# Two value products, the scale of x and its split moved one step earlier in a fused attention and two-layer-pair kernel

## The chip, the cores and the metric

The kernel runs on one core of one Trainium2 chip. The metric is the device time of one execution in microseconds (us); the kernel before takes 1294.16 us (median of three runs, 1293.89 to 1294.37). TensorE (PE) does the matrix products, ScalarE (ACT) and VectorE (DVE) the work on their results, GpSimd (POOL) part of the subtractions, and SyncE (SP) issues the DMAs.

## The reference

An attention of 12,288 query tokens over 768 keys, which serve as values too, is followed by two feed-forward pairs of width 2048:

```
kv_pool = kv.reshape(B, H // r, r, W // r, r, C).mean(axis=(2, 4))
k = v = kv_pool.reshape(B, -1, C) @ w_sr
a = softmax(q @ k.T / sqrt(C));   x = a @ v
h = x @ w_in;   g = max(h, 0) + alpha * min(h, 0);   x = g @ w_out
h = x @ w_in2;  g = h * sigmoid(1.702 * h);          out = g @ w_out2
```

C is 128, so q and x have 128 columns. All is float32 at the surface.

## The kernel before, in words

Every float32 operand is split in two float16 parts, high and low, and each product is three matmuls (high by high, high by low, low by high), all recorded at lines 103, 104 and 105. Ahead of a split a power of two is found from the largest absolute value, so that the parts keep their precision.

The 12,288 tokens are 24 blocks of 512, numbered 0 to 23. A block's 2048 hidden columns are 16 pieces of 128. One loop over steps t runs all blocks as a pipeline, 16 steps to a block. Block j's first layer stands at steps 16j to 16j+15, one piece in each; its second layer comes 4 steps later, the third 31 and the fourth 36 steps later. A step in the middle of the program thus works on three or four blocks at once. The text uses these short names:

- L1 m, L2 m, L3 m, L4 m: the three matmuls of piece m in one of the four layers. L1 and L3 write a tile `h` in PSUM, L2 and L4 add up in a tile `y`.
- A1 m (line 346) and A3 m (line 401): the ScalarE function on `h`. D1 m (line 347) and D3 m (line 402): the VectorE operation behind it, the last reader of that `h`. H1 m (354) and H3 m (409): ScalarE's cast to the high part. P1 m (355) and P3 m (411): the subtraction that gives the low part, on GpSimd, or on VectorE for P3 of every fourth piece.
- S n: the scores of the next block's n-th tile of 128 queries (lines 236 to 240). The work behind it is a maximum on VectorE (`nm`, line 245), the exponential on ScalarE (255), the scaled high part `ah` on ScalarE (269), the low part `al` on VectorE (280), and a DMA transpose of each.
- V k: the k-th of six products with the values, which add up x in the PSUM tile `xacc`.

Between V 5 and the first layer of the same block stands the chain that this case is about. `top_of` reduces `xacc` on VectorE (`ta`, line 304) and writes a column `xd`. `x_scale` has TensorE spread `xd` over the partitions with a matmul of one column (`pt`, line 309), and VectorE makes the scale `xc` of it (`xp`, `xc`). `x_split` writes the high part `xh` on ScalarE (320) and the low part `xl` on VectorE (321). L1 0 of the block reads `xh` and `xl`.

The matmul `pt` writes a tile of the same PSUM pool `ps_h` as L1 and L3. It has three buffers, handed out in the order in which the code asks for them. So `pt` takes a place in that row, and the L1 and L3 that stand around it need the buffers of pieces that are nearer to them.

Which step holds what is written in tables: `ATT_START` gives the step at which a block's attention begins (16j-25 for block j), `ATT_S` the places of its four S, `ATT_V` those of its six V, and the loop in `step` has the lags of `x_scale` and `x_split`. The code of the steps is then ordered once more by a scheduler that moves an instruction ahead where it expects the one before it to wait. Each engine gets a fixed list and works it in that order; an instruction that waits holds all behind it on its engine.

The lines that the change touches:

Of the kernel before, what the change touches and what calls it, by code (L numbers as in the profile page):

```python
# [27 lines left out]
KF = DFF // P  # L28
TB = 512
NB = NTOK // TB  # L30
# [7 lines left out]
L2_LAG, L3_LAG, L4_LAG = 4, 31, 36  # L38

ATT_START = [-18, -5] + [KF * j - 25 for j in range(2, NB)]  # L40
ATT_S = [(0, 2, 2, 6), (0, 3, 6, 9)] + [(0, 4, 7, 12)] * (NB - 2)
ATT_V = [(5, 8, 9, 12), tuple(range(12, 18))] + [(17, 18, 19, 21, 22, 22)] * (NB - 2)
KV_FREE = -11
W4_LOAD = -8

# [8 lines left out]
def attn_moe_kernel(ctx: ExitStack, tc: tile.TileContext, q, kv, w_sr, w_in1, w_out1, alpha, w_in2, w_out2, out):  # L54
# [47 lines left out]
    def mm3(o, wh, wl, xh, xl, start, stop):  # L102
        mm(out=o, lhsT=wh, rhs=xh, start=start, stop=False)  # L103
        mm(out=o, lhsT=wh, rhs=xl, start=False, stop=False)  # L104
        mm(out=o, lhsT=wl, rhs=xh, start=False, stop=stop)  # L105
# [7 lines left out]
    def small(name, dt=F32, w=1):  # L113
        return sm_p.tile([P, w], dt, tag=name, name=name)
# [90 lines left out]
    def flush():  # L205
        while late:
            late.pop(0)()
# [3 lines left out]
    def a_q(j):  # L211
        d = small("qd", BF16)
        top_of(q_t[j], d)
        qsc[j] = d

    def q_split(j):
        src = q_t.pop(j)
        qh[j] = at_p.tile([P, TB], F16, tag="qh", name="qh")
        ql[j] = at_p.tile([P, TB], F16, tag="ql", name="ql")
        c, p = scale_of(qsc[j], ps_x.tile([P, TB], F32, tag="x", name="qt"), None, "q")  # L220
        qsc[j] = p
        late.append(lambda: parts(qh[j], ql[j], src, c))
# [27 lines left out]
    def a_e(j, t):  # L250
        d = st[j, t]

        e = e_p.tile([P, 2, HALF], F32, tag="e", name="e") if j < 2 else d["s"][:, :, 0:HALF]
        sm = at_p.tile([P, 1], F32, tag="sm", name="sm")
        nc.scalar.activation(e, d["s"][:, :, 0:HALF], AF.Exp, bias=d["nm"], scale=qsc[j], accum_out=sm)  # L255
        r = at_p.tile([P, 1], F32, tag="r", name="r")
        d["e"], d["r"] = e, r

        def f():

            nc.vector.tensor_scalar(out=r, in0=sm, scalar1=1e-9, scalar2=2.0 ** -15, op0=ALU.add, op1=ALU.mult)
            nc.vector.reciprocal(out=r, in_=r)

        late.append(f)

    def a_h(j, t):
        d = st[j, t]
        d["ah"] = e_p.tile([P, 2, HALF], F16, tag="ah", name="ah")
        nc.scalar.activation(d["ah"], d["e"], AF.Copy, scale=d["r"])
        if t == 0:  # L270
            eh[j] = at_p.tile([P, KT, TB], F16, tag="eh", name="eh")
            el[j] = at_p.tile([P, KT, TB], F16, tag="el", name="el")
        nc.sync.dma_start_transpose(out=eh[j][:, :, t * P:(t + 1) * P], in_=d["ah"].rearrange("p h k -> p (h k)"))

    def a_l(j, t):
        d = st.pop((j, t))
        lo = e_p.tile([P, 2, HALF], F16, tag="al", name="al_")

        def f():
            nc.vector.scalar_tensor_tensor(out=lo, in0=d["e"], scalar=d["r"], in1=d["ah"], op0=ALU.mult, op1=ALU.subtract)  # L280
            nc.sync.dma_start_transpose(out=el[j][:, :, t * P:(t + 1) * P], in_=lo.rearrange("p h k -> p (h k)"))

        late.append(f)

    def a_v(j, k):
        if k == 0:
            xacc[j] = ps_x.tile([P, TB], F32, tag="x", name="xacc")
        if j == 0:

            ts_ = slice(k * P, (k + 1) * P)  # L290
            for i in range(KT):
                mm3(xacc[j][:, ts_], v_hi[:, i, :], v_lo[:, i, :], eh[j][:, i, ts_], el[j][:, i, ts_],
                    i == 0, i == KT - 1)
        else:
            mm3(xacc[j], v_hi[:, k, :], v_lo[:, k, :], eh[j][:, k, :], el[j][:, k, :], k == 0, k == KT - 1)
        if k == len(ATT_V[j]) - 1:
            d = small("xd", BF16)
            xsc[j] = d
            late.append(lambda: top_of(xacc[j], d))
# [36 lines left out]
    def l1(j, m):  # L336
        h = ps_h.tile([P, TB], F32, tag="h", name="h1")
        ms = slice(m * P, (m + 1) * P)
        mm3(h, wh["w1"][:, ms], wl["w1"][:, ms], xh[j], xl[j], True, True)
        h1[j, m] = h  # L340
# [9 lines left out]
    def l1_split(j, m):  # L350
        hi = g_p.tile([P, TB], F16, tag="g1h", name="g1h")
        lo = g_p.tile([P, TB], F16, tag="g1l", name="g1l")
        g = gg.pop((j, m, 1))
        nc.scalar.copy(hi, g)  # L354
        nc.gpsimd.tensor_tensor(out=lo, in0=g, in1=hi, op=ALU.subtract)  # L355
        g1[j, m] = hi, lo

    def l2(j, m):
        if m == 0:
            y1[j] = ps_y.tile([P, TB], F32, tag="y", name="y1")  # L360
        hi, lo = g1.pop((j, m))
        ms = slice(m * P, (m + 1) * P)
        mm3(y1[j], wh["w2"][:, ms], wl["w2"][:, ms], hi, lo, m == 0, m == KF - 1)
        if m == KF - 1:
            y = y1.pop(j)
            yc[j] = at_p.tile([P, TB], F32, tag="yc", name="yc", bufs=1)
            d = small("yd", BF16)
            ysc[j] = d

            def f():  # L370

                nc.scalar.copy(yc[j], y)
                top_of(y, d)

            late.append(f)
# [21 lines left out]
    def l3_act(j, m):  # L397
        h = h3.pop((j, m))
        g = t_p.tile([P, TB], F32, tag="g2", name="g2", bufs=3)

        nc.scalar.activation(g, h, AF.Tanh, scale=ysc[j][:, 0:1])  # L401
        nc.vector.scalar_tensor_tensor(out=g, in0=g, scalar=1.0, in1=h, op0=ALU.add, op1=ALU.mult)  # L402
        gg[j, m, 2] = g

    def l3_split(j, m):
        hi = g_p.tile([P, TB], F16, tag="g2h", name="g2h")
        lo = g_p.tile([P, TB], F16, tag="g2l", name="g2l")
        g = gg.pop((j, m, 2))
        nc.scalar.copy(hi, g)  # L409
        e = nc.vector if j == 0 or m % 4 == 3 or j == NB - 1 and m % 2 else nc.gpsimd  # L410
        e.tensor_tensor(out=lo, in0=g, in1=hi, op=ALU.subtract)  # L411
        g2[j, m] = hi, lo

    def l4(j, m):
        if m == 0:
            y2[j] = ps_y.tile([P, TB], F32, tag="y", name="y2")
        hi, lo = g2.pop((j, m))
        ms = slice(m * P, (m + 1) * P)
        mm3(y2[j], wh["w4"][:, ms], wl["w4"][:, ms], hi, lo, m == 0, m == KF - 1)
        if m == KF - 1:  # L420
            ob = t_p.tile([P, TB], F32, tag="ob", name="ob")
            y = y2.pop(j)
            u = ysc.pop(j)

            def f():
                nc.scalar.activation(ob, y, AF.Copy, scale=u[:, 1:2])
                nc.sync.dma_start(out=out[:, j * TB:(j + 1) * TB], in_=ob)

            late.append(f)
# [104 lines left out]
    def at(t, lag):  # L534

        j, m = divmod(t - lag, KF)
        return (j, m) if 0 <= j < NB else None

    def step(t):
        pieces = [(j, t - ATT_START[j]) for j in range(NB) if -8 < t - ATT_START[j] < 26]  # L540
        if x := at(t, L2_LAG):
            l2(*x)
        flush()
        if x := at(t, 2):
            l1_split(*x)
        if x := at(t, L3_LAG + 1):
            l3_act(*x)
        if x := at(t, L3_LAG + 2):
            l3_split(*x)
        if x := at(t, 0):  # L550
            l1(*x)
        if x := at(t, L4_LAG):
            l4(*x)
        flush()
        for j, p in pieces:
            for n, p0 in enumerate(ATT_S[j]):
                if p == p0 + 1:
                    a_e(j, n)
                elif p == p0 + 2:
                    a_h(j, n)  # L560
                elif p == p0 + 3:
                    a_l(j, n)
        flush()
        for j, p in pieces:
            for n, p0 in enumerate(ATT_S[j]):
                if p == p0:
                    a_s(j, n)
            for k, p0 in enumerate(ATT_V[j]):
                if p == p0:
                    a_v(j, k)  # L570
            if p == -6 and j > 0:
                a_q(j)
            if p == -4 and j > 0:
                q_split(j)
                late.append(lambda j=j: q_scale(j))
                if j + 1 < NB:
                    load_q(j + 1)
        for f, lag in ((x_scale, -2), (x_split, -1), (y_scale, L2_LAG + KF), (y_split, L2_LAG + KF + 2)):
            if (x := at(t, lag)) and x[1] == 0:
                f(x[0])  # L580
        if x := at(t, L3_LAG):
            l3(*x)
        if x := at(t, 0):
            l1_act(*x)
        flush()
# [59 lines left out]
```

## Time and profile before

| | |
|---|---|
| time, median of 3 runs | 1294.16 us |
| the profiled execution: time, span | 1294.28 us, 1292.5 us |
| TensorE busy | 1228.2 us, 95% of the span |
| VectorE, ScalarE, GpSimd busy | 1036.0, 1107.2, 780.6 us |
| mean granted TensorE clock | 0.979 of full speed |

TensorE is busy nearly all the time after a start of some 150 us, and the other engines have gaps. But the length that the profile gives a matmul (0.38 us for 512 columns) overlaps the next one: a row of 512 columns starts 0.216 us after the one before it where nothing holds it. A wait of less than the overlap does not show as idle time; it shows as a start that is further from the last start than that. So the waits of the middle are read from the starts in the timeline, not from the table of waits.

### The profile page before, as it was taken

What the parts mean: (1) busy time and instruction counts of PE and PEld (TensorE: products, weight loads), DVE (VectorE), ACT (ScalarE), POOL (GpSimd) and SP (SyncE); (2) the same over time, 40 slices, a digit from 0 to 9 for tenths busy, and PEclk for the clock granted to TensorE, in tenths of its full rate; (3) what the DMA queues carried; (4) which work ended last, traced back from release to release, by engine and by line L of the source; (5) the groups of instructions that cost most, each with busy time, mean ns of one, the idle gap of its engine ahead of it and who ended that gap; (6) DMA issues with size and microseconds to landing.
All of it is one profiled execution on the core that took longest, in us unless ns stands there. A gap on an engine that the chain in (4) does not pass through costs nothing.

```text
span 1292.5 us, 18032 instructions
## 1 busy us (share of the span) xinstructions
PE 1228.2 (95%) x5784; PEld 567.1 (44%) x5784; DVE 1036.0 (80%) x1879; ACT 1107.2 (86%) x1964; POOL 780.6 (60%) x670
## 2 busy tenths in 40 slices
PE   3468999999999999999999999999999999999998
PEld 2323444444444444444444444444444444444443
DVE  7988899778788787887887787787888878877666
ACT  1477899899898898898898998998988988988998
POOL 1046535576675676666665665756756666667774
PEclk8678999999999999999999999999999999999999
DMA  9713312122121221211221121221212212110000
GB/s 374 169 43 56 62 33 54 37 41 54 25 54 42 37 54 33 45 42 37 48 48 38 42 54 30 49 47 32 53 33 46 49 32 43 34 37 21 9 9 17
DMA packets 165375, 66.65 MB, mean 52 GB/s; under 512 B 156448, under 2 KB 156576, under 8 KB 164256
## 3 DMA queue, kind: packets, MB, share of 16 engines
q1 hardware_dynamic: 165280, 65.51, 21.9%
q8 instruction: 45, 0.74, 0.2%
q14 instruction: 50, 0.41, 0.1%
HBM read 21.05 MB, written 6.29 MB: 21 GB/s over the span
## 4 chain that ended last, share of the span: by engine, by line
PE 55%; ACT 16%; DVE 13%; issue 5%; DMA 0%; POOLq 0%; ACTq 0%
PE h L103 8%; PE h L105 7%; PE h L104 7%; PE y L104 7%; PE y L105 7%; PE y L103 7%; DVE g L347 4%; ACT g L346 4%; ACT g L401 3%; ACT s L255 3%; DVE g L402 2%; ACT g1h L354 2%; PE xacc L103 2%; PE xacc L104 2%; PE xacc L105 2%
## 5 line engine op out<-in xcount | busy, mean ns | idle before, releaser
L355 POOL TENSOR_TENSOR g1l<-g,g1h 128x512 f16<-128x512 f32 x384 | 457.0, 1196 | 324.9 <-ACT g1h L354 308.8
L411 POOL TENSOR_TENSOR g2l<-g,g2h 128x512 f16<-128x512 f32 x272 | 315.4, 1160 | 120.5 <-ACT g2h L409 110.9
L401 ACT ACTIVATE g<-h,yu 128x512 f32<-128x512 f32 x384 | 269.4, 702 | 103.9 <-PE h L105 100.8
L402 DVE SCALAR_TENSOR_TENSOR g<-g,h 128x512 f32<-128x512 f32 x384 | 262.5, 684 | 110.6 <-ACT g L401 104.9
L347 DVE SCALAR_TENSOR_TENSOR g<-g,oma,h 128x512 f32<-128x512 f32 x384 | 284.9, 742 | 53.1 <-ACT g L346 47.1
L354 ACT CAST g1h<-g 128x512 f16<-128x512 f32 x384 | 244.3, 637 | 7.2 <-PE y L105 5.6
L346 ACT ACTIVATE g<-h 128x512 f32<-128x512 f32 x384 | 236.2, 615 | 15.3 <-PE h L105 8.0
L409 ACT CAST g2h<-g 128x512 f16<-128x512 f32 x384 | 243.8, 635 | 3.3 <-PE y L105 1.2
L104 PE MATMUL y<-g1l,w2h 128*128 128x512 f16 x384 | 145.5, 379 | 8.7 <-POOL g1l L355 8.7
L103 PE MATMUL h<-xh,w1h 128*128 128x512 f16 x384 | 146.5, 383 | 5.2 <-ACT xh L320 4.1
L103 PE MATMUL h<-yh,w3h 128*128 128x512 f16 x384 | 145.2, 378 | 4.2 <-DVE g L347 1.1
L104 PE MATMUL h<-xl,w1h 128*128 128x512 f16 x384 | 146.6, 382 | 1.4
L105 PE MATMUL h<-xh,w1l 128*128 128x512 f16 x384 | 146.7, 382 | 0.0
L103 PE MATMUL y<-g1h,w2h 128*128 128x512 f16 x384 | 145.6, 379 | 1.2 <-ACT g1h L354 1.2
L104 PE MATMUL y<-g2l,w4h 128*128 128x512 f16 x384 | 145.5, 379 | 0.5 <-POOL g2l L411 0.5
L105 PE MATMUL y<-g2h,w4l 128*128 128x512 f16 x384 | 145.5, 379 | 0.0
L105 PE MATMUL y<-g1h,w2l 128*128 128x512 f16 x384 | 145.5, 379 | 0.0
L103 PE MATMUL y<-g2h,w4h 128*128 128x512 f16 x384 | 145.5, 379 | 0.0
L105 PE MATMUL h<-yh,w3l 128*128 128x512 f16 x384 | 145.4, 379 | 0.0
L104 PE MATMUL h<-yl,w3h 128*128 128x512 f16 x384 | 145.3, 378 | 0.0
L245 DVE TENSOR_REDUCE nm<-s 128x1 f32<-128x768 f32 x96 | 91.5, 953 | 14.2 <-PE s L240 10.6
L411 DVE TENSOR_TENSOR g2l<-g,g2h 128x512 f16<-128x512 f32 x112 | 90.0, 804 | 9.7 <-ACT g2h L409 9.7
(227 smaller groups left out, 1664.8 us busy)
## 6 DMA issues: line engine op xcount, KB each, us to landing
q<-in_q SPq DMA_DIRECT2D x24, 256.0 KB, 2.6
kv<-in_kv SPq DMA_DIRECT2D x12, 512.0 KB, 9.9
out<-ob SPq DMA_DIRECT2D x24, 256.0 KB, 2.0
raw_w<-in_moe_w_in SPq DMA_DIRECT2D x4, 1024.0 KB, 9.7
raw_w<-in_moe_w_out SPq DMA_DIRECT2D x4, 1024.0 KB, 6.9
eh<-ah SPq DMA_TRANSPOSE x96, 2.7
wsr<-in_w_sr SPq DMA_DIRECT2D x1, 64.0 KB, 2.7
al<-in_moe_alpha SPq DMA_DIRECT2D x1, 8.0 KB, 1.8
```

The lines of the kernel that those rows point to most:

```text
L103: mm(out=o, lhsT=wh, rhs=xh, start=start, stop=False)
L104: mm(out=o, lhsT=wh, rhs=xl, start=False, stop=False)
L105: mm(out=o, lhsT=wl, rhs=xh, start=False, stop=stop)
L245: nc.vector.tensor_reduce(out=nm, in_=s[:, :, 0:HALF], axis=AX.XY, op=ALU.max, negate=True)
L346: nc.scalar.activation(g, h, AF.Relu, scale=-1.0)
L347: nc.vector.scalar_tensor_tensor(out=g, in0=g, scalar=oma[:, m:m + 1], in1=h, op0=ALU.mult, op1=ALU.add)
L354: nc.scalar.copy(hi, g)
L355: nc.gpsimd.tensor_tensor(out=lo, in0=g, in1=hi, op=ALU.subtract)
L401: nc.scalar.activation(g, h, AF.Tanh, scale=ysc[j][:, 0:1])
L402: nc.vector.scalar_tensor_tensor(out=g, in0=g, scalar=1.0, in1=h, op0=ALU.add, op1=ALU.mult)
L409: nc.scalar.copy(hi, g)
L411: e.tensor_tensor(out=lo, in0=g, in1=hi, op=ALU.subtract)
```

## The change

The last three of the six V of blocks 2 to 23 go from places 21, 22, 22 to 20, 21, 21: they are V 3, V 4 and V 5. V 3 now stands in the step of S 1 of the next block, one step sooner. For all 24 blocks `x_scale` goes from two steps to three ahead of the block's first layer, and `x_split` from one step to two.

```
-ATT_V = [(5, 8, 9, 12), tuple(range(12, 18))] + [(17, 18, 19, 21, 22, 22)] * (NB - 2)
+ATT_V = [(5, 8, 9, 12), tuple(range(12, 18))] + [(17, 18, 19, 20, 21, 21)] * (NB - 2)
...
-        for f, lag in ((x_scale, -2), (x_split, -1), (y_scale, L2_LAG + KF), (y_split, L2_LAG + KF + 2)):
+        for f, lag in ((x_scale, -3), (x_split, -2), (y_scale, L2_LAG + KF), (y_split, L2_LAG + KF + 2)):
```

The lists of the engines hold the same instructions in number and kind. The order on SP is the same. On TensorE, in the middle of the program (here ahead of block 5), the place of `pt` before is behind S 2 and ahead of L3 15:

```order
L240 LDWEIGHTS ql
L240 MATMUL s<-k_hi,ql 128x384
L309 LDWEIGHTS ones
L309 MATMUL pt<-xd,ones 128x1
L103 LDWEIGHTS w3h
L103 MATMUL h_3155<-yh,w3h 128x512
L104 LDWEIGHTS w3h
L104 MATMUL h_3155<-yl,w3h 128x512
```

And now, at the same boundary, it is behind L4 9 (`y<-g2h,w4l`), with two of the three matmuls of L2 10 (`y<-g1h`, `y<-g1l`) and then L3 14 behind it:

```order
L105 LDWEIGHTS w4l
L105 MATMUL y_2769<-g2h,w4l 128x512
L309 LDWEIGHTS ones
L309 MATMUL pt<-xd,ones 128x1
L103 LDWEIGHTS w2h
L103 MATMUL y_2750<-g1h,w2h 128x512
L104 LDWEIGHTS w2h
L104 MATMUL y_2750<-g1l,w2h 128x512
L103 LDWEIGHTS w3h
L103 MATMUL h_3116<-yh,w3h 128x512
```

With it, V 3 stands ahead of S 1, and V 4 and V 5 behind L4 8. Between V 5 and `pt` there were L3 14, L2 10, L1 14, L4 10 and S 2; now there are L3 13, L2 9, L1 13 and L4 9. The order of L1 0 and L4 12 (before: one matmul of L1 0, one of L4 12, then the rest) is now plain.

On VectorE the same place reads before as follows; `g2l` is P3 11, `al` belongs to S 1, line 402 is D3 (13, then 14 behind `xd`), line 347 D1 13:

```order
L411 TENSOR_TENSOR g2l<-g_3011,g2h 128x512
L280 SCALAR_TENSOR_TENSOR al__3140<-s,r,ah 128x768
L402 SCALAR_TENSOR_TENSOR g_3085<-g_3085,h_3071 128x512
L347 SCALAR_TENSOR_TENSOR g_3113<-g_3113,oma,h_3092 128x512
L304 TENSOR_REDUCE ta<-xacc 128x1
L304 TENSOR_REDUCE ta<-q_2733 128x1
L109 TENSOR_SCALAR xd<-ta 128x1
L402 SCALAR_TENSOR_TENSOR g_3126<-g_3126,h_3109 128x512
```

And now:

```order
L411 TENSOR_TENSOR g2l<-g_3011,g2h 128x512
L304 TENSOR_REDUCE ta<-xacc 128x1
L280 SCALAR_TENSOR_TENSOR al__3146<-s,r,ah 128x768
L109 TENSOR_SCALAR xd<-ta 128x1
L402 SCALAR_TENSOR_TENSOR g_3095<-g_3095,h_3078 128x512
L347 SCALAR_TENSOR_TENSOR g_3120<-g_3120,oma,h_3102 128x512
L109 TENSOR_SCALAR xp<-pt 128x1
L304 TENSOR_REDUCE ta<-q_2733 128x1
L111 TENSOR_SCALAR xc<-xp,kxc 128x1
L109 TENSOR_SCALAR qd<-ta 128x1
L402 SCALAR_TENSOR_TENSOR g_3132<-g_3132,h_3116 128x512
L321 SCALAR_TENSOR_TENSOR xl<-xacc,xc,xh 128x512
```

The reduction of `xacc` and `xd` have gone ahead of D3 13 and D1 13, and `xl` stands ahead of S 2's `nm`, where it stood behind D1 15.

## Rows read from the trace of the kernel before

**Rows 1.** The page: busy time of each engine, its share, instructions.

```profile
PE 1228.2 (95%) x5784; PEld 567.1 (44%) x5784; DVE 1036.0 (80%) x1879; ACT 1107.2 (86%) x1964; POOL 780.6 (60%) x670
```

**Rows 2.** Stretches: length; busy PE, PEld, DVE, ACT, POOL; granted clock, DMA share, GB/s.

```profile
100.00:150.00 50.00, 42.74 (x188) 18.44 (x186) 41.08 (x74) 37.78 (x65) 30.29 (x23) 0.95 0.28 53
150.00:200.00 50.00, 48.67 (x233) 22.07 (x232) 47.58 (x89) 44.25 (x80) 19.70 (x17) 1.00 0.22 46
550.00:600.00 50.00, 49.78 (x238) 22.92 (x237) 40.29 (x74) 44.99 (x81) 32.28 (x29) 1.00 0.20 43
```

**Rows 3.** Timeline, TensorE: start, length, line, operation; the scale matmuls of two blocks.

```profile
248.80 0.17 PE L309 MATMUL pt<-xd,ones 128*128 128x1 bf16 x1
...
1150.44 0.17 PE L309 MATMUL pt<-xd,ones 128*128 128x1 bf16 x1
```

**Rows 4.** Timeline, TensorE: the two waits at the boundary to block 5.

```profile
303.01 0.38 PE L103 MATMUL y<-g2h,w4h 128*128 128x512 f16 x1
303.47 0.38 PE L104 MATMUL h<-xl,w1h 128*128 128x512 f16 x1
...
306.92 0.38 PE L103 MATMUL y<-g1h,w2h 128*128 128x512 f16 x1
307.32 0.38 PE L103 MATMUL h<-yh,w3h 128*128 128x512 f16 x1
```

**Rows 5.** Timeline, VectorE: x's low part ahead of block 5, and later rows.

```profile
302.67 0.74 DVE L321 SCALAR_TENSOR_TENSOR xl<-xacc,xc,xh 128x512 f16<-128x512 f32 x1
...
305.92 0.68 DVE L411 TENSOR_TENSOR g2l<-g,g2h 128x512 f16<-128x512 f32 x1
...
306.52 0.74 DVE L347 SCALAR_TENSOR_TENSOR g<-g,oma,h 128x512 f32<-128x512 f32 x1
```

**Rows 6.** Timeline, TensorE: from S 1's end to V 3, and around `pt`.

```profile
288.20 0.38 PE L103 MATMUL h<-yh,w3h 128*128 128x512 f16 x1
...
290.79 0.38 PE L103 MATMUL xacc<-eh,v_hi 128*128 128x512 f16 x1
...
298.89 0.17 PE L309 MATMUL pt<-xd,ones 128*128 128x1 bf16 x1
298.92 0.38 PE L103 MATMUL h<-yh,w3h 128*128 128x512 f16 x1
```

**Rows 7.** Timeline, VectorE: from P3 11 to D3 14.

```profile
292.32 1.23 DVE L411 TENSOR_TENSOR g2l<-g,g2h 128x512 f16<-128x512 f32 x1 [0.28 <-ACT g2h L409]
293.47 1.00 DVE L280 SCALAR_TENSOR_TENSOR al__3140<-s,r,ah 128x768 f16<-128x768 f32 x1
294.39 0.67 DVE L402 SCALAR_TENSOR_TENSOR g<-g,h 128x512 f32<-128x512 f32 x1
...
295.65 0.68 DVE L304 TENSOR_REDUCE ta<-xacc 128x1 f32<-128x512 f32 x1
296.25 0.67 DVE L304 TENSOR_REDUCE ta<-q 128x1 f32<-128x512 f32 x1
296.84 0.14 DVE L109 TENSOR_SCALAR xd<-ta 128x1 bf16<-128x1 f32 x1
296.91 0.68 DVE L402 SCALAR_TENSOR_TENSOR g<-g,h 128x512 f32<-128x512 f32 x1
```

**Rows 8.** Timeline, ScalarE: S 1's exponential and H3 11.

```profile
289.70 0.96 ACT L255 ACTIVATE s<-s,nm,qu 128x768 f32<-128x768 f32 x1
...
291.65 0.63 ACT L409 CAST g2h<-g 128x512 f16<-128x512 f32 x1
```

**Rows 9.** Timeline, VectorE: `xd` of block 0.

```profile
65.31 0.14 DVE L109 TENSOR_SCALAR xd<-ta 128x1 bf16<-128x1 f32 x1
```

**Rows 10.** Timeline, TensorE: block 0's `pt`, and block 1's first L1.

```profile
65.50 0.19 PE L309 MATMUL pt<-xd,ones 128*128 128x1 bf16 x1 [1.95 <-DVE xd L109]
...
120.05 0.81 PE L103 MATMUL h<-xh,w1h 128*128 128x512 f16 x3 [1.19 <-ACT xh L320]
```

**Rows 11.** Timeline, GpSimd: P1 11 beside P3 11.

```profile
291.84 1.16 POOL L355 TENSOR_TENSOR g1l<-g,g1h 128x512 f16<-128x512 f32 x1 [2.56 <-ACT g1h L354]
```

## The prediction

> **What bounds the kernel now.** I read the page first: TensorE is busy for 95% of the span, the next engine for 86% [rows 1]. The table of stretches then shows two parts. From about 200 us on TensorE is busy 49.78 of every 50 us, at a granted clock of 1.00, the 2.4 GHz level; ahead of that it has 42.74 and 48.67 in two stretches [rows 2]. So the middle goes at TensorE's pace, and only a wait on TensorE costs there.
>
> The third view is TensorE's timeline. The scale matmul `pt` of block 4 starts at 248.80 and that of block 22 at 1150.44 [rows 3]: 18 blocks in 901.64 us, 50.09 us each. Then I looked for starts that stand further apart than the streaming time. Four groups of three matmuls take 290.79 - 288.20 = 2.59 us [rows 6], so a group is 0.6475 us and a matmul 0.216. At the boundary to block 5 two starts are late: 303.47 - 303.01 - 0.216 = 0.24 us and 307.32 - 306.92 - 0.216 = 0.18 us [rows 4]. The first waits for `xl`, which VectorE ends at 302.67 + 0.74 = 303.41 [rows 5]. The second is L3 2. The buffer order gives it that of L1 0, which D1 0 frees at 306.52 + 0.74 = 307.26 [rows 5]. I call them the old waits; they come back at the same place of each block.
>
> **The change part by part.** Nothing is added or taken away, so the cost is waits alone. The same 24 `pt`, `xp`, `xc`, `xh` and `xl` run. No moved step issues a DMA, and SP's order stays. GpSimd now has P3 13 ahead of P1 13; L2 13 and L4 13 use them some ten groups (6 us) later, with room for the 1.16 us of one such operation [rows 11], so I cost that at nothing.
>
> First old wait: with the split a step sooner `xl` stands ahead of S 2's maximum on VectorE, and from `pt` to L1 0 TensorE has ten groups and S 2. My count below leaves `xl` some 4 us early. That is -0.24 per block.
>
> New wait: `pt` needs `xd`, and `xd` sits in VectorE's list behind P3 11 (`g2l`), `ta` and `al`. I count from the end of S 1, which the row of the next matmul gives as 288.20 [rows 6].
> - VectorE to P3 11: 292.32 - 288.20 = 4.12 [rows 6, 7]. The work between is S 1's maximum, its exponential (289.70) and then ScalarE's list to H3 11 (291.65) [rows 8], with P3 11 right behind it. This chain hangs on S 1's end alone. V 3 now stands ahead of S 1, so all of it comes 0.65 later in the program, and 4.12 stays.
> - Behind P3 11: to the next operation 293.47 - 292.32 = 1.15; `ta` 296.25 - 295.65 = 0.60; `al` 294.39 - 293.47 = 0.92 [rows 7]. `xd` starts at 4.12 + 1.15 + 0.60 + 0.92 = 6.79.
> - From `xd`'s start to `pt`: 65.50 - 65.31 = 0.19 [rows 9, 10]. `pt` can start at 6.98.
> - TensorE from S 1's end to `pt`: L3 12, L2 8, L1 12, L4 8, V 4, V 5, L3 13, L2 9, L1 13, L4 9, ten groups, 6.48.
>
> So `pt` waits 0.50 us. Before, `xd` ended at 296.98 and `pt` started at 298.89 [rows 6, 7], 1.9 us in hand: S 2 and a group stood between, and `ta` found D3 13 and D1 13 done.
>
> Behind `xd` comes D3 13, at 6.79 + 296.91 - 296.84 = 6.86, for 0.68 [rows 7]. With `pt` in the row of buffers L3 14 needs the buffer of L3 13, so it can start at 6.86 + 0.68 + 0.06 = 7.60; 0.06 is what lies between D1 0's end and L3 2 (307.32 - 307.26 [rows 4, 5]). Without any wait TensorE would come there at 6.48 + 0.03 for `pt` (298.92 - 298.89 [rows 6]) + two matmuls 0.43 = 6.94. So L3 14 is 0.66 late, and the 0.50 at `pt` is part of it. Both waits hang on the same VectorE list. L1 14 needs D1 13, which starts 0.60 behind D3 13 and takes some 0.75: 8.25 with the same 0.06, against 7.60 + 0.86 = 8.46 on TensorE, no wait. Behind that S 2 (about 1 us) gives cover.
>
> Second old wait: TensorE comes to L3 2 later by 0.66 - 0.24 and sooner by 0.22, because two matmuls of L2 14 no longer stand ahead of it: 0.20 later. On VectorE the list from S 2 to D1 0 starts about 0.7 later and loses `xl` (0.74). The bounds are nothing and the present 0.18; I take 0.10, as the two shifts nearly cancel.
>
> Here a rule of the Trainium skill bears on a term. P3 11 takes 1.23 us at 292.32, while GpSimd's P1 11 runs from 291.84 to 293.00 [rows 7, 11]; a like one with no GpSimd operation beside it takes 0.68 [rows 5]. The page "SBUF — State Buffer", section "SBUF: two separate sides", says that VectorE with two SBUF inputs and GpSimd share a port as an exclusive lock, and the later one is held. The rows agree in size (293.00 + 0.55 = 293.55).
>
> P1 11 and P3 11 both hang on ScalarE's list behind the same exponential, and both move by the same 0.65, so I keep 1.15 for the distance; the other end is 0.60, as of an operation that meets none, and it is a rival below.
>
> Sum for one boundary: +0.66 + 0.10 - 0.24 - 0.18 = +0.34 us. Blocks 3 to 22 have it: the nineteen from row 248.80 to row 1150.44, and block 3, whose lists read the same there; its other duties differ and I take the same value. 20 x 0.34 = +6.8 us. At block 23 no S follows, VectorE has neither `nm` nor `al` there, and I count nothing.
>
> The start (blocks 0 to 2) can't be read so cleanly: VectorE has 41 to 48 of 50 us there [rows 2], and its work is the same. Block 1's first L1 waits 1.19 us for `xh` [rows 10]. That wait gone is -1.2; one more of that size is +1.2. I take zero.
>
> The profiled execution took 1294.28 us (span 1292.5 and 1.8 around it), 0.1 above the median of 1294.16, which I neglect. 1294.3 + 6.8 = 1301.1 us.
>
> **The rivals.**
> - VectorE keeps up. If `xd` is there when TensorE comes, both old waits go and none comes: -0.42 x 20 = -8.4, 1285.9 us. For it speaks the 1.9 us that `pt` has in hand now; against it that this room came from the pieces that no longer stand between, and that the new order of VectorE puts P3 11 and `al` ahead of `xd`. 8%.
> - P3 11 no longer meets P1 11. VectorE's list is then 0.55 shorter: `pt` does not wait, L3 14 waits 0.11, and a boundary comes to 0.11 + 0.10 - 0.42 = -0.21, in all -4.2: 1290.1 us. Against it: both hang on the same exponential. 5%. By the page on the SBUF this lock is what decides.
> - The wait is only exchanged. If the chain from S 1's end to P3 11 shortens by 0.3 where V 3's move leaves ScalarE gaps, the new wait is about 0.36, with 0.06 left of the second old one: no change, 1294.3 us. A change within 0.2% (2.6 us, about what a measurement tells from none) falls here. For it: ScalarE has slack, 44.99 of 50 us [rows 2]. Against it: each link of the chain waits for the one before it, not for a free engine. 10%.
> - Slower still. If the later P3 15 at 305.92 (0.68 now [rows 5]) meets a GpSimd operation, it takes 0.55 more and D1 0 with it; the second wait becomes about 0.65 and a boundary costs 0.66 + 0.65 - 0.42 = +0.89: 1312 us. It decides where GpSimd's subtraction starts ahead of VectorE's. 7%.
>
> **How the numbers follow.** The forecast has 70%. Its own range: the new wait 0.56 to 0.76 (five rounded distances), the second 0 to 0.18, so +0.14 to +0.52 per boundary or 2.8 to 10.4 in all; few of these ends meet, so with the 1.2 of the start it is 1297 to 1305.5 us. I widen it down to 1293.8, which takes in the exchange; what is left out is the two faster cases and the slowest, 20%. Faster by more than 0.2%: 8 + 5% = 13%. Within: 10% and 1% of the forecast's low end, 11%. Slower: 69 + 7 = 76%.
>
> **What would show it.** In the profile after, `pt` in the middle should start about 0.5 us later than L4 9 ends, right behind `xd`, and L3 14 right behind D3 13. L1 0's second matmul should follow without a gap and `xl` end some 4 us ahead of it. The period of `pt` should be 50.4 us in place of 50.09. A period of 49.7 would say that VectorE keeps up; a VectorE P3 11 of 0.68 us that the lock decided; a gap of over 0.5 us at L3 2 the slowest case. A change that shows ahead of 200 us and not in the period would make the whole count wrong.

## The result and the profile after

The changed kernel takes 1301.17 us (median of four runs, 1299.25 to 1302.52) against 1294.03 (median of four runs of the kernel before, with one more than the three above): a ratio of 1.0052, 95% interval 1.0039 to 1.0065. It is slower by 7.1 us; 1301.1 was forecast. That the forecast is met to 0.1 us is luck: the four runs lie 3.3 us apart, and the profiled execution (1301.79 us) is 7.5 us longer than the one before.

The page of the changed kernel has the same work as before [rows 1]: busy time of each engine, its share, instructions.

```profile
PE 1229.4 (95%) x5784; PEld 566.2 (44%) x5784; DVE 1035.5 (80%) x1879; ACT 1110.1 (85%) x1964; POOL 781.9 (60%) x670
```

Its table of stretches (columns as in [rows 2]) shows TensorE 0.25 us less busy in a stretch of the middle:

```profile
550.00:600.00 50.00, 49.53 (x237) 22.81 (x236) 39.85 (x73) 45.15 (x81) 31.99 (x28) 1.00 0.20 43
```

TensorE's timeline, with the scale matmuls of blocks 4 and 22 (in brackets the idle time ahead and what ended it):

```profile
246.54 0.16 PE L309 MATMUL pt<-xd,ones 128*128 128x1 bf16 x1 [0.35 <-DVE xd L109]
...
1154.54 0.16 PE L309 MATMUL pt<-xd,ones 128*128 128x1 bf16 x1 [0.34 <-DVE xd L109]
```

18 blocks take 908.00 us, 50.44 each, where it was 50.09 [rows 3]: +0.35 us. Twenty such boundaries are 7.1 us. The boundary to block 5 on TensorE, from the end of S 1 (the first row starts there):

```profile
290.00 0.38 PE L103 MATMUL h<-yh,w3h 128*128 128x512 f16 x1
...
296.26 0.38 PE L105 MATMUL y<-g2h,w4l 128*128 128x512 f16 x1
296.98 0.16 PE L309 MATMUL pt<-xd,ones 128*128 128x1 bf16 x1 [0.34 <-DVE xd L109]
...
297.22 0.38 PE L104 MATMUL y<-g1l,w2h 128*128 128x512 f16 x1
297.58 0.38 PE L103 MATMUL h<-yh,w3h 128*128 128x512 f16 x1
...
304.59 0.38 PE L103 MATMUL h<-xh,w1h 128*128 128x512 f16 x1
304.81 0.38 PE L104 MATMUL h<-xl,w1h 128*128 128x512 f16 x1
...
308.26 0.38 PE L105 MATMUL y<-g2h,w4l 128*128 128x512 f16 x1
308.61 0.38 PE L103 MATMUL h<-yh,w3h 128*128 128x512 f16 x1
```

The streaming time of 0.216 us taken off each distance, `pt` is 0.50 us late (296.26 to 296.98) and L3 14 another 0.14 (297.22 to 297.58). L1 0's second matmul (304.81) follows its first at 0.22, so the first old wait is gone. L3 2 is 0.13 late (308.26 to 308.61), where it was 0.18 [rows 4]. Together 0.50 + 0.14 + 0.13 - 0.24 - 0.18 = +0.35. The bracket at `pt` says 0.34 only, since the length given for the matmul ahead of it covers 0.16 of the wait.

VectorE's timeline of the same stretch:

```profile
294.11 1.23 DVE L411 TENSOR_TENSOR g2l<-g,g2h 128x512 f16<-128x512 f32 x1 [0.28 <-ACT g2h L409]
295.27 0.68 DVE L304 TENSOR_REDUCE ta<-xacc 128x1 f32<-128x512 f32 x1
295.87 1.00 DVE L280 SCALAR_TENSOR_TENSOR al__3146<-s,r,ah 128x768 f16<-128x768 f32 x1
296.79 0.14 DVE L109 TENSOR_SCALAR xd<-ta 128x1 bf16<-128x1 f32 x1
296.85 0.67 DVE L402 SCALAR_TENSOR_TENSOR g<-g,h 128x512 f32<-128x512 f32 x1
...
299.75 0.74 DVE L321 SCALAR_TENSOR_TENSOR xl<-xacc,xc,xh 128x512 f16<-128x512 f32 x1
...
307.81 0.74 DVE L347 SCALAR_TENSOR_TENSOR g<-g,oma,h 128x512 f32<-128x512 f32 x1
```

`xl` ends at 299.75 + 0.74 = 300.49, 4.3 us ahead of the matmul that reads it. Counted from 290.00, P3 11 starts at 4.11, `ta` at 5.27, `al` at 5.87 and `xd` at 6.79; 0.19 behind it `pt` starts. D3 13 ends at 297.52 and L3 14 starts 0.06 later. P3 11 is 1.23 us long again, for GpSimd's P1 11 is beside it:

```profile
293.64 1.16 POOL L355 TENSOR_TENSOR g1l<-g,g1h 128x512 f16<-128x512 f32 x1 [3.21 <-ACT g1h L354]
```

The rest is in the start. Block 1's first L1 waits 1.57 us for `xh`, where it was 1.19 [rows 10]; but it starts 0.13 us sooner than before (119.92 and 120.05), and other waits of the start have changed too, so the runs show no single one as the cause:

```profile
119.92 0.59 PE L103 MATMUL h<-xh,w1h 128*128 128x512 f16 x2 [1.57 <-ACT xh L320]
```

S 1 of this boundary ends at 290.00, 1.80 us later than before [rows 6]. 0.65 of it is V 3, which now stands ahead. The L4 8 behind S 1 is late by 1.05 us ahead of block 3 and by 1.80 ahead of block 5, so the boundaries of blocks 3 and 4 make 0.75, and the other 0.40 us came before them. With the 7.1 us of the twenty boundaries that makes 7.5 us, the difference of the two spans (1300.0 and 1292.5).

### The profile page after: what moved, and what is told of

Same layout as the page of the kernel before. It is cut to its first block, busy times and chain, and to the rows that moved or that the text cites. A ratio compares the mean times of both kernels' runs of the same rounds, so it can differ in the third digit from the quotient of the medians.

```text
span 1300.0 us, 18011 instructions
## 1 busy us (share of the span) xinstructions
PE 1229.4 (95%) x5784; PEld 566.2 (44%) x5784; DVE 1035.5 (80%) x1879; ACT 1110.1 (85%) x1964; POOL 781.9 (60%) x670
## 4 chain that ended last, share of the span: by engine, by line
PE 58%; DVE 14%; ACT 8%; issue 3%; POOLq 0%; ACTq 0%
PE h L103 9%; PE h L105 8%; PE h L104 8%; PE y L103 8%; PE y L104 8%; PE y L105 8%; DVE g L347 3%; ACT s L255 3%; ACT g L401 2%; DVE g L402 2%; DVE ta L304 2%; PE s L236 1%; PE s L240 1%; PE s L237 1%; PE xacc L104 1%
## 5 line engine op out<-in xcount | busy, mean ns | idle before, releaser
L409 ACT CAST g2h<-g 128x512 f16<-128x512 f32 x384 | 241.1, 628 | 4.3 <-PE y L105 1.2
L346 ACT ACTIVATE g<-h 128x512 f32<-128x512 f32 x384 | 232.6, 606 | 12.8 <-PE h L105 5.2
```

The costliest lines, as they stand in the source:

```text
L346: nc.scalar.activation(g, h, AF.Relu, scale=-1.0)
```

## The experiments

The theory is the forecast's: `pt` in its new place comes ahead of `xd`, because VectorE's list behind S 1 is not through, and the two old waits are the gain that is set against it. The rivals are named with each run. Part m stands for the subtraction P3 m, which makes the low part of piece m of the fourth layer's input. Single runs of one kernel spread by several us (25 runs of the kernel before from 1292.4 to 1298.1), so each is read by its median, by the ratio, and by the period of `pt` from block 4 to block 22 in its profile, which holds the boundaries alone.

**The values alone.**

```
+ATT_V = ... [(17, 18, 19, 20, 21, 21)] * (NB - 2)     # lags of x_scale, x_split as before: -2, -1
```

> V 3, V 4 and V 5 at their new places, x's scale and split at the lags of the kernel before. Theory (the new loss is pt and L3 14 waiting for a VectorE list that is late for the new place of pt): pt stands again behind S 2, with L3 14, L2 10, L1 14, L4 10 and S 2 between V 5 and it, some 3.6 us, so it does not wait; the two old waits of 0.24 and 0.18 us stay. About 1294 us (1293 to 1295.5), period of pt 50.09 us. Rival (V 3 ahead of S 1, which puts S 1's softmax work 0.65 us later, is what costs): 1298 to 1301 us without the scale being moved.

1295.96 us against 1294.28, ratio 1.0009 (0.9999 to 1.0018). `pt` starts at 250.89 and 1152.72, a period of 50.10. It does not wait; the old waits are there with 0.23 and 0.18 us. The median is 0.5 us above the expected range. `pt` of block 4 comes 2.1 us later than before (250.89 and 248.80), so what is above came ahead of that, and behind it V 3 ahead of S 1 costs nothing while `pt` stands behind S 2. The theory holds, and the rival falls.

**The split alone.**

```
-        for f, lag in ((x_scale, -2), (x_split, -1), ...
+        for f, lag in ((x_scale, -2), (x_split, -2), ...
```

> The values and the scale as in the kernel before, only x's split one step sooner (same step as the scale). Theory: no wait at pt. xl is done before L1 0 comes, so the first old wait (0.24 us) goes; but L3 2 then comes 0.24 us sooner to the buffer that D1 0 frees, and D1 0 hangs on a list of ScalarE and VectorE that does not move, so the second old wait grows from 0.18 to about 0.4 us. About 1294 us (1292.5 to 1295), period 50.09. Rival (the split's lateness is a cost by itself): 0.24 us x 20 blocks = 4.8 us less, 1289.5 us, period 49.85.

1294.64 us, ratio 0.9997 (0.9986 to 1.0008), period (1151.08 - 249.54) / 18 = 50.09. The wait of L1 0 is gone. L3 2 on TensorE's timeline:

```profile
507.77 0.38 PE L103 MATMUL y<-g1h,w2h 128*128 128x512 f16 x1
508.39 0.38 PE L103 MATMUL h<-yh,w3h 128*128 128x512 f16 x1 [0.25 <-DVE g L347]
```

508.39 - 507.77 - 0.216 = 0.40 us, where it was 0.18. Of the 0.24 us taken at one place 0.22 came back 4 us later at the next: D1 0 hangs on a list that the split does not shorten. The first old wait thus hid most of a longer second one, and the split alone is worth next to nothing.

**V 3 back behind S 1.**

```
-... [(17, 18, 19, 20, 21, 21)] * (NB - 2)
+... [(17, 18, 19, 21, 21, 21)] * (NB - 2)
```

> The changed kernel, but V 3 one step later, beside V 4 and V 5 and behind S 1 as in the kernel before; scale and split stay moved. Theory, by the same count from S 1's end: al now ahead of ta, ta starts at 6.19, D3 13 next at 6.79, xd at 7.39, pt can start at 7.58; TensorE has eleven groups, 7.12 us, so pt waits about 0.45 us; L3 14 behind it does not wait again. Old first wait gone, second about 0.1: +0.1 to +0.2 us per block, 1296 to 1299 us. Rival (V 3 ahead of S 1 is the cause): both old waits gone and no new one, 1286 to 1289 us. Second rival (only the row of the three PSUM buffers counts): as the changed kernel, 1301 us.

1303.24 us, ratio 1.0063 (1.0045 to 1.0081): slower than any of the three answers. Its TensorE rows, first 508 to 512 us and then at `pt`:

```profile
510.54 0.38 PE L105 MATMUL y<-g1h,w2l 128*128 128x512 f16 x1
511.19 0.38 PE L103 MATMUL h<-xh,w1h 128*128 128x512 f16 x1 [0.27 <-DVE g L402]
...
547.99 0.38 PE L105 MATMUL y<-g2h,w4l 128*128 128x512 f16 x1
548.67 0.16 PE L309 MATMUL pt<-xd,ones 128*128 128x1 bf16 x1 [0.30 <-DVE xd L109]
```

`pt` waits 0.46 us, as counted. But L1 2, at 511.19, waits 0.43 us for D3 1, which the count did not have. On VectorE and GpSimd ahead of it:

```profile
508.87 1.67 DVE L411 TENSOR_TENSOR g2l<-g,g2h 128x512 f16<-128x512 f32 x1
...
510.46 0.67 DVE L402 SCALAR_TENSOR_TENSOR g<-g,h 128x512 f32<-128x512 f32 x1
```

```profile
508.83 2.73 POOL L355 TENSOR_TENSOR g1l<-g,g1h 128x512 f16<-128x512 f32 x2 [1.14 <-ACT g1h L354]
```

P3 15 starts 0.04 us behind a GpSimd subtraction and takes 1.67 us in place of 0.68 [rows 5]. That is the mechanism that the forecast named for its slowest case, but with 0.99 us more where it had 0.55, and with the wait at L1 2 where it had L3 2. 0.46 + 0.43 - 0.42 = 0.47 per block, 9.4 us in all; 9.0 were measured.

**VectorE's low parts one piece earlier.**

```
-        e = nc.vector if j == 0 or m % 4 == 3 or ...
+        e = nc.vector if j == 0 or m % 4 == 2 or ...
```

> The changed kernel, but of every four low parts of the fourth layer's input VectorE makes the third and not the last: P3 10 in place of P3 11, P3 14 in place of P3 15; as many instructions on each engine. Theory: P3 10 comes in VectorE's free time ahead of S 1's maximum, so the list behind S 1 is 1.15 us shorter: xd is there when TensorE comes to pt, L3 14 waits 0 to 0.2 us for D3 13, and D1 0 is earlier, so the old second wait goes too: -0.2 to -0.4 us per block against the kernel before, 1286 to 1291 us. Rival (the PSUM buffers' row or the place of V 3 costs, not the VectorE list): 1299 to 1302 us as the changed kernel.

1296.01 us, ratio 1.0009 (0.9997 to 1.0021): outside the range. `pt` does not wait any more (547.94, no bracket), L3 14 waits 0.13 us and L3 2 not at all, as the theory had it. The gain went at the scale of y (made for the third layer as that of x is for the first), where two waits of 0.06 and 0.29 us had stood; now there is one of 0.69 us:

```profile
523.07 0.38 PE L105 MATMUL y<-g2h,w4l 128*128 128x512 f16 x1
523.98 0.38 PE L103 MATMUL h<-yh,w3h 128*128 128x512 f16 x1 [0.53 <-DVE g L347]
```

0.13 + 0.69 against 0.24 + 0.18 + 0.06 + 0.29 is +0.05 per block, and the period is 50.16. So the VectorE list is what held `pt`, and parts 2 and 6 in place of 3 and 7 harmed another stretch; the next run keeps 3 and 7, and this wait is not there.

**Parts 3, 7, 10 and 14 on VectorE in the changed kernel.**

```
+        e = nc.vector if j == 0 or m in (3, 7, 10, 14) or ...
```

> The changed kernel, with VectorE making the low parts 3, 7, 10 and 14 of the fourth layer's input (before: 3, 7, 11, 15), so that the list behind S 1 and behind S 2 is shorter and the stretch around the scale of y is as it was. Theory: pt does not wait, L3 14 waits 0.13 us for D3 13, L1 0 and L3 2 do not wait, and the two waits further on (0.06 and 0.29 us) stay as before: period of pt 49.8 us, 1294.3 - 20 x 0.29 = about 1288.5 us (1287 to 1291). Rival (what is taken from one list comes back as a wait elsewhere, as in the run with parts 2, 6, 10, 14): 1293 to 1297 us.

1290.55 us against 1294.69, ratio 0.9971 (0.9962 to 0.9981): faster than both kernels. `pt` and its neighbours on TensorE, `xd` on VectorE, and the period:

```profile
543.62 0.38 PE L105 MATMUL y<-g2h,w4l 128*128 128x512 f16 x1
543.83 0.17 PE L309 MATMUL pt<-xd,ones 128*128 128x1 bf16 x1
544.00 0.38 PE L103 MATMUL h<-yh,w3h 128*128 128x512 f16 x1
```

```profile
543.21 0.15 DVE L109 TENSOR_SCALAR xd<-ta 128x1 bf16<-128x1 f32 x1
```

```profile
244.72 0.17 PE L309 MATMUL pt<-xd,ones 128*128 128x1 bf16 x1
...
1142.06 0.17 PE L309 MATMUL pt<-xd,ones 128*128 128x1 bf16 x1
```

`xd` ends 0.47 us ahead of `pt`, L3 14 waits 0.14, and the period is 49.85. The median is 2 us above the expected 1288.5 and inside the range.

**The same low parts in the kernel before.**

```
+        e = nc.vector if j == 0 or m in (3, 7, 10, 14) or ...     # tables and lags of the kernel before
```

> The kernel before with low parts 3, 7, 10 and 14 on VectorE, nothing else. Theory: L1 0 still waits 0.24 us for xl, the second old wait goes since D1 0 comes 0.6 us sooner: period 49.91 us, about 1290.7 us (1289.5 to 1292). Rival (exchanged again): 1294 us.

1293.24 us, ratio 0.9984 (0.9972 to 0.9996); period (1150.01 - 249.38) / 18 = 50.04. L3 2 does not wait, L1 0 waits 0.23. But of the 0.18 us gained 0.13 came back at the scale of y, where the wait of 0.06 is now 0.19. Expected was 1290.7 (1289.5 to 1292): a miss, since most of the gain was exchanged.

**Split sooner and the same low parts.**

```
+        for f, lag in ((x_scale, -2), (x_split, -2), ...
+        e = nc.vector if j == 0 or m in (3, 7, 10, 14) or ...
```

> The kernel before with x's split one step sooner and low parts 3, 7, 10 and 14 on VectorE; values and scale not moved. Theory: both old waits go and none comes: period 49.67 us, 1294.3 - 20 x 0.42 = about 1286 us (1285 to 1288). If the split's 0.24 us only comes back at L3 2 as in the run with the split alone: 1290 to 1291 us.

1292.72 us, ratio 0.9986 (0.9977 to 0.9995), period (1149.42 - 248.80) / 18 = 50.03. A miss: both old waits are gone, and 0.07 + 0.05 us behind L1 0 and 0.31 + 0.28 at the scale of y took nearly all of it. The profile names D1 (line 347) as what ended the wait of 0.31; what holds D1 up there was not tested.

**The split left at its old lag.**

```
-        for f, lag in ((x_scale, -3), (x_split, -2), ...
+        for f, lag in ((x_scale, -3), (x_split, -1), ...     # values as in the changed kernel
```

> The changed kernel with x's split at its old lag (one step ahead of the first layer); values and scale moved. Theory: the new waits hang on the place of pt and of V 3 to V 5 alone, and pt stands where it stands in the changed kernel; xl still ends some 3 us ahead of L1 0, since xc is there sooner. Waits of 0.5 at pt and 0.14 at L3 14 as in the changed kernel, period 50.4, 1300 to 1302.5 us. Rival (the earlier split holds D3 and D1 up and causes the loss): 1294 to 1297 us.

1308.46 us, ratio 1.0111 (1.0096 to 1.0126), a miss of 6 us upward. `pt` and L3 14 wait 0.51 and 0.13 us as in the changed kernel. L1 2 waits once more for D3 1, on TensorE, VectorE and GpSimd:

```profile
512.90 0.38 PE L105 MATMUL y<-g1h,w2l 128*128 128x512 f16 x1
513.60 0.38 PE L103 MATMUL h<-xh,w1h 128*128 128x512 f16 x1 [0.32 <-DVE g L402]
```

```profile
511.28 1.68 DVE L411 TENSOR_TENSOR g2l<-g,g2h 128x512 f16<-128x512 f32 x1
```

```profile
511.25 1.16 POOL L355 TENSOR_TENSOR g1l<-g,g1h 128x512 f16<-128x512 f32 x1 [1.74 <-ACT g1h L354]
```

P3 15 starts 0.03 us behind the GpSimd operation and takes 1.68 us. Of the blocks 4 to 22 it is so in 18 (1.67 or 1.68 us), and in one, block 10, it falls the other way: GpSimd is held (1.73 us) and VectorE is not.

```profile
562.06 1.73 POOL L355 TENSOR_TENSOR g1l<-g,g1h 128x512 f16<-128x512 f32 x1 [1.74 <-ACT g1h L354]
```

```profile
562.09 0.69 DVE L411 TENSOR_TENSOR g2l<-g,g2h 128x512 f16<-128x512 f32 x1
```

There L1 2 does not wait (563.71 to 563.93), and the block takes 50.33 us, where its neighbours take 50.81. Neither theory nor rival had this; the next but one run tests it too.

**Only part 15 off the list, in the changed kernel.**

```
+        e = nc.vector if j == 0 or m in (3, 7, 11, 14) or ...
```

> The changed kernel with VectorE making low part 14 in place of 15 (3, 7, 11, 14): the list behind S 1, on which pt hangs, is left as it is, the list behind S 2 loses P3 15. Theory: pt waits 0.50 and L3 14 another 0.14 us as in the changed kernel; the wait of 0.13 at L3 2 goes. Period about 50.3 us, 1298 to 1300.5 us. Rival (the earlier gain came from part 15 and not from part 11): 1289 to 1292 us as in the run with parts 3, 7, 10, 14.

1298.86 us, ratio 1.0028 (1.0016 to 1.0040). `pt` still waits 0.51 us and L3 14 0.13:

```profile
548.18 0.38 PE L105 MATMUL y<-g2h,w4l 128*128 128x512 f16 x1
548.91 0.16 PE L309 MATMUL pt<-xd,ones 128*128 128x1 bf16 x1 [0.35 <-DVE xd L109]
```

The wait at L3 2 is gone; the period is (1152.72 - 246.72) / 18 = 50.33, and 0.51 + 0.13 - 0.42 = 0.22 of it above 50.09. Between this run and the one with part 10 in place of part 11 lie 0.48 us per block (50.33 and 49.85): P3 11 ahead of `xd` is what the new wait hangs on.

**Only part 15 off the list, with the split unmoved.**

```
+        e = nc.vector if j == 0 or m in (3, 7, 11, 14) or ...
+        for f, lag in ((x_scale, -3), (x_split, -1), ...
```

> The run with x's split at its old lag, and low part 14 on VectorE in place of 15. Theory: the 0.48 us at L1 2 came from P3 15 on VectorE, which overlaps a GpSimd operation there and takes 1.68 us; without it that wait goes, pt and L3 14 keep 0.51 and 0.13: period about 50.3 us, 1298 to 1301 us. Rival (the place of xl and xh in the lists made that wait): 1306 to 1309 us as before.

1298.24 us against 1308.46 of the run with part 15; the ratio to the kernel before is 1.0034 (1.0024 to 1.0044), where it was 1.0111:

```profile
245.29 0.16 PE L309 MATMUL pt<-xd,ones 128*128 128x1 bf16 x1 [0.35 <-DVE xd L109]
...
1151.39 0.16 PE L309 MATMUL pt<-xd,ones 128*128 128x1 bf16 x1 [0.35 <-DVE xd L109]
```

The period is 50.34, where it was 50.80 with part 15 on VectorE, and L1 2 waits no more. So that wait came from P3 15 on VectorE, not from the place of `xl`; that it is GpSimd's hold on P3 15, and not a longer list, block 10 of the run with part 15 shows. L1 0 does not wait for `xl` either, though the split is at its old lag (`xl` ends at 552.07, and the matmul that reads it starts at 555.32). Split moved or not, the kernel is the same then (50.33 and 50.34): the split had no part in the loss, and the first old wait goes without it.

## Why the prediction was right, step by step

- The new wait was counted at 0.50 at `pt` and 0.66 by L3 14; it is 0.50 and 0.64. That it hangs on VectorE's list behind S 1 is shown: the list shortened by P3 11 (parts 10 and 14 run) takes the wait at `pt` away, and the list shortened elsewhere (part 14 for 15) does not.
- The first old wait went, as forecast, but the reason given, the split a step sooner, was not needed: with the split at its old lag it is gone too, since `pt` and with it `xc` come sooner. What that is worth was taken too singly. The split alone gave 0.24 us at L1 0 and lost 0.22 at L3 2. In the sum this did no harm, since the second old wait had a term of its own: 0.10 against 0.13 measured. The 0.22 by which TensorE comes sooner to L3 2 is one matmul, not two as the forecast says: only `y<-g1h` stood between [rows 4].
- P3 11 kept its 1.23 us beside P1 11, so 1.15 was the right end of that term. By the page "SBUF — State Buffer" of the Trainium skill, section "SBUF: two separate sides", the port pair that VectorE and GpSimd share is an exclusive lock. The runs agree: a P3 with no GpSimd operation beside it takes 0.68 us (P3 3 at 317.16 in the kernel before; the P3 15 of [rows 5] meets one 0.63 us behind its start), and P3 15 takes 1.67 and 1.68 where it starts 0.04 and 0.03 us behind a GpSimd subtraction of 1.16. At 0.03 us the order of the rows does not settle which of the two is held: in block 10 of the run with the split unmoved it was GpSimd, with 1.73 us in place of 1.16. No run took P1 11 away alone, so how much of the wait at `pt` this hold of P3 11 makes is counted (0.55 of its list) and not shown.
- The twenty boundaries are 7.1 us against 6.8, and the start +0.40 against zero within 1.2: in the profiled execution 7.5 against 6.8. That the median came closer still is the luck named above.
- That each boundary begins alike, whatever the one before it lost, was taken for granted; the same waits at every block and the even period show it.
- Of the rivals the slowest, a P3 15 that meets GpSimd, did not come in the changed kernel: P3 15 started at 307.20 for 0.69 us, ahead of a GpSimd operation at 307.77. It came in two variants that differ from the changed kernel by one step of one operation, for 0.43 and 0.48 us a block; the forecast's 0.55 for the hold was too small there, since P3 15 started right behind the start of the GpSimd operation and lost 0.99 and 1.00.

## What to carry to other kernels

Ahead of moving an operation one step sooner, count what stands ahead of its input on the engine that makes it, and what the engine that waits has left between the two: here 6.98 us against 6.48. A wait taken away is a gain only if the next one does not hang on a list that stays as it was. Where TensorE is full, look for waits in the distances of its starts, since each of them here was partly or wholly hidden in the length that the profile gives a matmul.

## What the runs showed that was not expected

A VectorE subtraction of two SBUF tiles whose row starts some 0.03 us behind that of a GpSimd one lost about 1 us in 18 of 19 blocks (4 to 22 of the run with the split unmoved); in block 10 it lost nothing, and GpSimd lost 0.57 us. One that starts 0.57 us ahead loses nothing. This chance of order, which no table of the kernel sets, is worth 0.48 us a block (50.81 against 50.33) in one and the same execution, an estimated 9.6 us over twenty blocks.
